# Two 32x32 products per head, moved from two strips of the PE array to four

## The chip, the cores and the metric

The kernel runs on one core of a Trainium2 chip. The metric is the time of one execution on the device, in microseconds (us). A core has TensorE (PE, matrix products; its weight loads are listed as PEld), VectorE (DVE), ScalarE (ACT), GpSimd (POOL) and SyncE (SP). SP, ACT and POOL also issue DMAs, each from a queue of its own. Every engine takes its instructions in order.

## The reference

The inputs are q, k, v of 4 batches, 8 heads, 768 tokens and 48 features, and beta. Per batch and head a delta rule runs over the tokens:

```
k_n = k / (norm(k) + 1e-6)
for t in range(S):
    y[t] = q[t] @ state
    state += beta[t] * outer(k_n[t], v[t] - k_n[t] @ state)
```

The 4 x 768 rows of 384 results then pass two layers: `relu(x @ w_in)**2 @ w_out` (384 to 2048 and back), and `max(x @ w1, x @ w2, x @ w3) @ w_out2` (384 to 768 and back).

## The kernel before, in words

The tokens are cut into 12 chunks (c) of 64. Within a chunk the delta rule needs, for each of 32 batch-head pairs, the inverse of a 64x64 triangular matrix with a unit diagonal. The pairs are held as 16 units u, with t = 0, 1 on the partitions: partition 64 t + token, then u.

The inverse is made in halves. `solve32` inverts the two 32x32 diagonal blocks of all pairs of two chunks at once on DVE (`solve`, lines 285 to 288) and stores them to DRAM as `xt` (line 325), one half h after the other. `load_x(c)` fetches them into `xb`: the first half to partitions 64 t to 64 t + 31, columns 0 to 31, the second half to the next 32 partitions, columns 32 to 63 (four DMAs, line 342). It also fetches `k21`, the off-diagonal block of the products of the keys (two DMAs, line 339; chunk 0 has that block in `kss`). For chunk 0 the DMAs are issued by SP and ACT, for the others by POOL.

The missing quarter is merged by two functions of `attention(c)`. `zz` transposes the first halves into `xT` on DVE (line 398), multiplies the second half by the off-diagonal block into `pZ` (line 405, 32 matmuls) and reads `pZ` out with the sign turned (lines 408, 410) into `z`, which is `k21`'s buffer. `ww` multiplies that by the first half into `pW` (line 418, 32 matmuls) and reads it out into `xb`, columns 32 to 63 of the first halves (lines 421, 423). In `pZ` and `pW` the units lie side by side on 32 partitions for each t:

```python
for u in range(B * Q):
    for t in range(2):
        pe.matmul(pW[first(t), u], xT[first(t), u], z[first(t), u], start=True, stop=True)
```

After that `mm_u` (line 449) applies the whole inverse, `st2` makes the outputs and the growth of the state (lines 489, 467), and `st3` transposes into `xh`, `xl`, the input of the first layer. `st0` (lines 428, 439, 442) stands ahead of it. Each runs once for either half p of the units. `load_att` issues on POOL's queue, behind `load_x`, the loads kq, v, p and ktp of a chunk (lines 358 to 366).

The first layer of chunk c (`moe_a(c)`, lines 544 and 562 on PE, 548 to 551 behind it: `gh` on ACT, `gl` on DVE) is interleaved with `attention(c + 1)`: `steps` takes some steps of the attention for each step of the layer, at given rates, and in even chunks a solve for the next two chunks beside them. PSUM holds two buffers for the layer's first product (`p1`), which come free with `gl`. The instruction lists that come out of this text are then ordered for each engine by the framework's planner, which simulates when data are ready. After chunk 11 the second layer runs (lines 849 to 869).

`behind(a, b)` only fixes an order of two instructions. `att` tiles with `bufs=1` have one buffer, which the next chunk takes over.

Of the kernel before, what the change touches and what calls it, by code (L numbers as in the profile page):

```python
# [8 lines left out]
F32 = mybir.dt.float32  # L9
# [4 lines left out]
AF = mybir.ActivationFunctionType  # L14
ALU = mybir.AluOpType
# [3 lines left out]
B, H, S, D = 4, 8, 768, 48  # L19
C = 64  # L20
NC = S // C
Q = H // 2
# [14 lines left out]
U2 = 2 * Q  # L37


def delta_moe(ctx, tc, kc, ab, kt, vt, beta, beta32, beta16, kq, w_in, w_out, w1, w2, w3, w_out2, out):  # L40
    nc = tc.nc
    vec, act, pool, pe = nc.vector, nc.scalar, nc.gpsimd, nc.tensor
# [11 lines left out]
    att = pr.enter_context(tc.tile_pool(name="att", bufs=2, side="right"))  # L54
    ps_at = pp.enter_context(tc.tile_pool(name="ps_at", bufs=3, space=PSUM))
# [12 lines left out]
    xt_d = [dram.tile([2, 2, B * Q, 32, 32], F32, name=f"xt{c}", tag=f"xt{c}") for c in range(NC)]  # L68
# [202 lines left out]
    def behind(ins, before):  # L271

        tc.add_manual_dep(ins, before.name, mybir.DependencyInfo(mybir.DependencyClass.NoSync, mybir.DependencyReason.DATA), reason="order")
# [55 lines left out]
    xb = st.tile([128, B * Q, C], F32, name="xb", tag="xb")  # L329
# [3 lines left out]
    def load_x(c):  # L333

        k21 = att.tile([128, B * Q, 32], F32, name="k21", tag="k21", bufs=1)
        ds = []
        for t in range(2):
            if c:
                ds.append(pool.dma_start(k21[64 * t + 32:64 * t + 64], kk_d[c][32:64, t, :, 0:32]))
            for h in range(2):  # L340
                o, hs = 64 * t + 32 * h, slice(32 * h, 32 * h + 32)
                i = (pool if c else (nc.sync, act)[t]).dma_start(xb[o:o + 32, :, hs], xt_d[c][h, t].rearrange("u j i -> j u i"))
                if c:
                    ds.append(i)
                else:
                    x_loaded.append(i.ins)
        for i in x_after:
            for d in ds:
                behind(d.ins, i)
        return k21  # L350

    def load_att(c, p):
        ds = []
        us = slice(U2 * p, U2 * p + U2)
        kq_ = None
        if c:
            kq_ = att.tile([R2, U2, 2, C], F32, name="kq", tag="kq")
            ds.append(pool.dma_start(kq_, two(kc, c, p).rearrange("p b q t s -> p (b q) t s")))
        v = att.tile([128, U2, D], F32, name="v", tag="v")
        ds.append(pool.dma_start(v, two(vt, c, p).rearrange("p b q d -> p (b q) d")))  # L360
        pt_ = masked.pop((c, p), None)
        if pt_ is None:
            pt_ = att.tile([128, U2, C], F32, name="p", tag="p")
            ds.append(pool.dma_start(pt_, p_d[c][:, us]))
        kt_ = ktp[p]
        ds.append(pool.dma_start(kt_[:, 0:U2 * D], two(kt, c, p).rearrange("p b q d -> p (b q d)")))
        for i in x_after:
            for d in ds:
                behind(d.ins, i)
        tiles[c, p] = [kq_, v, xb[:, us], pt_, kt_, None, None, None, None]  # L370

    xh, xl, masked, last_act, last_vec = {}, {}, {}, [None], [None]
# [3 lines left out]
    def attention(c):  # L376
# [3 lines left out]
        first = lambda t: slice(64 * t, 64 * t + 32)  # L380
        last = lambda t: slice(64 * t + 32, 64 * t + 64)
# [10 lines left out]

        merge = []

        def zz(k21):
            xT = att.tile([128, B * Q, 32], F32, name="xT", tag="xT", bufs=1)
            z = k21
            last_vec[0] = vec.transpose(out=xT, in_=xb[:, :, 0:32]).ins
            if c == 1:
                behind(last_vec[0], last_gl[0])  # L400
            pZ = ps_at.tile([128, B * Q, 32], F32, name="pZ", tag="at")
            for u in range(B * Q):
                for t in range(2):
                    lower = k21[last(t), u] if c else kss[u // U2][last(t), 0, u % U2, 0:32]
                    pe.matmul(pZ[first(t), u], lower, xb[last(t), u, 32:64], start=True, stop=True)  # L405
            for t in range(2):
                if t and not c:
                    last_vec[0] = vec.tensor_scalar(out=z[first(t)], in0=pZ[first(t)], scalar1=-1.0, scalar2=None, op0=ALU.mult).ins
                else:
                    last_act[0] = act.activation(out=z[first(t)], in_=pZ[first(t)], func=AF.Copy, scale=-1.0).ins  # L410
            merge.extend((xT, z))

        def ww(_):
            xT, z = merge
            pW = ps_at.tile([128, B * Q, 32], F32, name="pW", tag="at")
            for u in range(B * Q):
                for t in range(2):
                    pe.matmul(pW[first(t), u], xT[first(t), u], z[first(t), u], start=True, stop=True)  # L418
            for t in range(2):
                if t and not c:  # L420
                    last_vec[0] = vec.tensor_copy(xb[first(t), :, 32:64], pW[first(t)]).ins
                else:
                    last_act[0] = act.copy(xb[first(t), :, 32:64], pW[first(t)]).ins

        def st0(p):
            kq_, v = tiles[c, p][0:2]
# [79 lines left out]
        def st3(p):  # L506
# [6 lines left out]
            last_act[0] = act.copy(hi, pv).ins  # L513
            last_vec[0] = vec.tensor_sub(out=xl[c][:, :, 128 * p:128 * (p + 1)], in0=pv, in1=hi.bitcast(F32)).ins  # L514

        k21 = load_x(c)
        if not c:
            load_att(c, 0)
        load_att(c, 1)
        if c:  # L520
            order = ((st0, 0),), ((zz, k21),), *(((),) if c == 1 else ()), ((ww, 0),), ((mm_u, 0),), ((st2, 0),), ((st0, 1), (st3, 0)), ((mm_u, 1),), ((st2, 1),), ((st3, 1),)
        else:
            order = ((st0, 0), (st0, 1)), ((zz, k21),), ((ww, 0),), ((mm_u, 0), (mm_u, 1)), ((st2, 0), (st2, 1)), ((st3, 0), (st3, 1)), ((state, 0), (state, 1))
        for fs in order:
            for f, p in fs:
                f(p)
                if f is (mm_u if c else state) and p and c + 1 < NC:
                    load_att(c + 1, 0)
            yield
# [121 lines left out]
    if True:  # L651
# [55 lines left out]
        at, p1 = (ps_at, "at"), (ps_s1, "p1")  # L707
# [47 lines left out]
        for f in range(NF):  # L755
            raw = fetch(wi_src[:, :, 256 * f:256 * (f + 1)], (KD, 128), nc.sync)
            t = None
            if f < NE:
                t = pkp.tile([128, KD, 128], I32, name=f"mag{f}", tag=f"mag{f}")
# [12 lines left out]
        for n, _ in zip((0, 2, 1, 1, 1, 1, 1), attention(0)):  # L772
            abs_after[:], cast_after[:] = cast_after or abs_after, [x for x in last_act if x]
            after[:] = [x for x in last_vec if x] or after
            words(n)
            if second_out:
                for x in second_out:
                    behind(nc.sync.dma_start(*x).ins, x_loaded[1])
                second_out.clear()
# [12 lines left out]
        for c in range(NC):  # L792
            extra = []
            if c + 1 < NC:
                extra.append((9 / 15.0, attention(c + 1)) if c > 1 else (13 / 15.0, later(3, attention(1))) if not c else (17 / 15.0, later(8, attention(2))))
# [24 lines left out]
            if c == NC - 1:  # L820
                pr.close()
                wb = ctx.enter_context(tc.tile_pool(name="wb", bufs=1, side="right", reuse_waits="tile"))
                first = []
# [117 lines left out]
```

## Time and profile before

| | |
|---|---|
| median of 3 runs | 995.46 us (994.43 to 995.75) |
| profiled execution | 997.21 us, its span 995.5 us |
| PE busy | 914.8 us, 92% of the span |
| DVE busy | 454.8 us, 46% |
| ACT busy | 420.1 us, 42% |
| POOL busy | 129.5 us, 13% |
| granted PE clock, mean | 0.958 of 2.4 GHz |
| DMA packets | 74916, of them 35520 under 512 B |

Times are of one profiled execution; the span runs from the first to the last instruction. A busy PE counts matmuls that overlap in the pipeline once. The name k in rows of the trace stands for the tile k21, p for the tile p or p1.

### The profile page before, as it was taken

Reading aid. Unit: us, or ns where it says so; the run is one execution under the profiler, and the core shown is the slowest. Engines: PE = TensorE matmul, PEld = TensorE weight load, DVE = VectorE, ACT = ScalarE, POOL = GpSimd, SP = SyncE. Lnnn points to the kernel's source line nnn. Section 1 sums busy time; section 2 is a strip of 40 time slices with the busy share of each in tenths; the row PEclk is TensorE's granted clock in tenths of the full one; section 3 lists DMA queues with packets and bytes.
Section 4 is the critical chain, followed back from the end, with each engine's and each line's share of the span. In section 5 each row is a group of like instructions: output and inputs, shape, how many; then the busy total and the mean of one; then the engine's idle time right before and its main releaser. Section 6 shows DMA issues by size and latency. Waiting matters only on the chain.

```text
span 995.5 us, 26545 instructions
## 1 busy us (share of the span) xinstructions
PE 914.8 (92%) x11674; PEld 841.1 (84%) x11674; DVE 454.8 (46%) x976; ACT 420.1 (42%) x805; POOL 129.5 (13%) x213
## 2 busy tenths in 40 slices
PE   5067878999999989999999799999999999999998
PEld 4057868999999989999999699999888888888887
DVE  2968577239423832384248234456732323232221
ACT  1946883444444444544444356555421212121111
POOL 3122311121121112112211111000200000000000
PEclk8567998999999999999999899999999999999999
DMA  9938822651564145414531532224500100000001
GB/s 203 315 87 246 238 71 62 150 163 53 135 163 103 53 133 150 117 53 134 150 80 55 138 100 78 66 80 127 159 9 16 47 16 32 16 17 16 12 21 40
DMA packets 74916, 97.25 MB, mean 98 GB/s; under 512 B 35520, under 2 KB 53232, under 8 KB 74800
## 3 DMA queue, kind: packets, MB, share of 16 engines
q1 hardware_dynamic: 54688, 54.22, 19.6%
q0 software_dynamic: 11584, 34.90, 12.6%
q10 hardware_dynamic: 8528, 6.42, 2.2%
q8 instruction: 92, 1.51, 0.7%
q14 instruction: 24, 0.20, 0.1%
HBM read 70.88 MB, written 24.64 MB: 96 GB/s over the span
## 4 chain that ended last, share of the span: by engine, by line
PE 69%; DVE 10%; issue 8%; DMA 6%; ACT 5%; POOL 1%; ACTq 0%; POOLq 0%; SPq 0%; DVEq 0%
PE p L849 23%; PE p L544 15%; PE px L562 15%; PE po L866 8%; DVE buf L287 3%; DVE buf L285 3%; DMA xb<-xt 2%; PE pU L449 2%; PE pZ L405 1%; DMA v<-in_vt_dram 1%; PE pY L489 1%; PE pW L418 1%; DMA xt<-buf 1%; PE pk L197 1%; DVE gl L551 1%
## 5 line engine op out<-in xcount | busy, mean ns | idle before, releaser
L562 PE MATMUL px<-gh,wout 128*128 128x256 f32 x1152 | 221.8, 290 | 1.7 <-issue 1.1
L849 PE MATMUL p<-x_h,w 128*128 128x512 f32 x648 | 203.5, 395 | 0.0
L562 PEld LDWEIGHTS px<-gh,wout 128*128 128x128 f32 x1152 | 181.6, 194 | 5.4 <-issue 1.0
L544 PE MATMUL p<-xh,win_h 128*128 128x256 f32 x576 | 170.5, 297 | 6.3 <-DVE gl L551 4.6
L544 PE MATMUL p<-xl,win_h 128*128 128x256 f32 x576 | 166.3, 292 | 2.8 <-DVE xl L514 2.8
L544 PE MATMUL p<-xh,win_l 128*128 128x256 f32 x576 | 165.5, 288 | 0.0
L562 PE MATMUL px<-gl,wout 128*128 128x256 f32 x576 | 163.9, 284 | 0.0
L849 PEld LDWEIGHTS p<-x_h,w 128*128 128x128 f32 x648 | 121.8, 188 | 27.0
L551 DVE TENSOR_TENSOR gl<-p,gh 128x512 fp32r<-128x512 f32 x96 | 65.7, 686 | 146.3 <-ACT gh L550 145.3
L849 PE MATMUL p<-x_l,w 128*128 128x512 f32 x324 | 128.1, 395 | 0.0
L548 ACT ACTIVATE p<-p 128x512 f32<-128x512 f32 x96 | 55.9, 582 | 156.8 <-PE p L544 155.6
L544 PEld LDWEIGHTS p<-xh,win_h 128*128 128x128 f32 x576 | 113.3, 197 | 10.1 <-DVE gl L551 5.5
L544 PEld LDWEIGHTS p<-xl,win_h 128*128 128x128 f32 x576 | 112.8, 197 | 3.9 <-DVE xl L514 2.9
L544 PEld LDWEIGHTS p<-xh,win_l 128*128 128x128 f32 x576 | 113.5, 197 | 0.1
L562 PEld LDWEIGHTS px<-gl,wout 128*128 128x128 f32 x576 | 111.4, 193 | 0.2 <-DVE gl L551 0.2
L855 DVE TENSOR_TENSOR mx<-p,mx 128x512 f32<-128x512 f32 x36 | 24.9, 691 | 127.2 <-PE p L849 127.1
L857 ACT CAST hh<-mx 128x512 fp32r<-128x512 f32 x36 | 22.3, 620 | 126.6 <-DVE mx L856 126.6
L849 PEld LDWEIGHTS p<-x_l,w 128*128 128x128 f32 x324 | 61.0, 188 | 14.5
L287 DVE TENSOR_TENSOR buf<-buf 128x30 f32<-128x30 f32 (+9 forms) x180 | 59.5, 331 | 5.2
L285 DVE TENSOR_TENSOR buf<-buf 128x30 f32<-128x30 f32 (+9 forms) x180 | 59.4, 330 | 5.4
L550 ACT CAST gh<-p 128x512 fp32r<-128x512 f32 x96 | 56.2, 585 | 2.7
L549 ACT ACTIVATE p<-p 128x512 f32<-128x512 f32 x96 | 55.9, 582 | 2.8
(171 smaller groups left out, 1338.1 us busy)
## 6 DMA issues: line engine op xcount, KB each, us to landing
kq<-in_kc_dram POOLq DMA_DIRECT2D x22, 448.0 KB, 4.4
raw<-in_moe_w_dram SPq DMA_DIRECT2D x18, 384.0 KB, 3.3
p<-p POOLq DMA_DIRECT2D x22, 256.0 KB, 3.3
raw<-in_moe_w_out_dram SPq DMA_DIRECT2D x14, 384.0 KB, 3.7
v<-in_vt_dram POOLq DMA_DIRECT2D x24, 192.0 KB, 4.2
ktp<-in_kt_dram POOLq DMA_DIRECT2D x24, 192.0 KB, 3.4
xr<-x SPq DMA_DIRECT2D x12, 384.0 KB, 3.1
out_dram<-os ACTq DMA_DIRECT2D x24, 192.0 KB, 1.9
```

Source lines behind the costliest of these rows:

```text
L285: eng.tensor_tensor(out=tv, in0=M[:, 0:j, j].unsqueeze(2).broadcast_to([u, j, m]), in1=M[:, j, j + 1:n].unsqueeze(1).broadcast_to([u, j, m ...
L287: yield eng.tensor_tensor(out=M[:, 0:j, j + 1:n], in0=M[:, 0:j, j + 1:n], in1=tv, op=ALU.add)
L544: pe.matmul(p1[:, j], w[:, k, f], x[c][:, k], start=n == 0 and j == 0, stop=n == 8, skip_group_check=True)
L548: act.activation(out=p1, in_=p1, func=AF.Relu)
L549: act.activation(out=p1, in_=p1, func=AF.Square)
L550: last_gh[0] = act.copy(gh, p1).ins
L551: last_gl[0] = vec.tensor_sub(out=gl, in0=p1, in1=gh.bitcast(F32)).ins
L562: pe.matmul(acc[m], w, x[:, j], start=f == 0 and i == 0 and m != 1, stop=f == NF - 1 and i == 2, skip_group_check=True)
L849: pe.matmul(p, w[i][:, k, fs], x[:, k], start=n == 0, stop=n == 8)
L855: vec.tensor_max(out=t, in0=ps[1], in1=t)
L857: act.copy(hh[:, f], t2)
L866: pe.matmul(po[:, 0:DM], x[:, f, js], w[:, f], start=i == 0, stop=i == 17)
```

## The change

Half of the units (u from 8 to 15) move beside the others on the partitions: `pZ`, `pW`, `xT` and `z` now have 8 units on 128 partitions instead of 16 on 64. Each matmul writes one of four 32-column strips; in `ww` it also reads from one of four 32-row strips. The order of the units alternates between the two groups. `z` is read out of `pZ` by one instruction on ACT instead of two, `pW` by four instead of two. As `xT` is now transposed from tiles on 128 partitions, the first halves are loaded a second time into a new tile `x1` in that layout, by four DMAs a chunk behind those of `xb`; the transpose takes `x1` instead of `xb`.

```diff
+        x1 = att.tile([128, U2, 32], F32, name="x1", tag="x1", bufs=1)
...
+        for t in range(2):
+            for g in range(2):
+                o = 64 * t + 32 * g
+                i = (pool if c else (nc.sync, act)[t]).dma_start(x1[o:o + 32], xt_d[c][0, t, U2 * g:U2 * g + U2].rearrange("u j i -> j u i"))
+                ds.append(i)
         for i in x_after:
-            for d in ds:
-                behind(d.ins, i)
-        return k21
+            if c:
+                for d in ds:
+                    behind(d.ins, i)
+        return k21, x1
...
+        part_ = lambda t, u: slice(64 * t + 32 * (u // U2), 64 * t + 32 * (u // U2) + 32)
+        spread = [u for v in range(U2) for u in (v, v + U2)]
+
+        def zz(k21, x1):
+            xT = att.tile([128, U2, 32], F32, name="xT", tag="xT", bufs=1)
+            z = k21[:, 0:U2]
+            last_vec[0] = vec.transpose(out=xT, in_=x1).ins
...
+            pZ = ps_at.tile([128, U2, 32], F32, name="pZ", tag="at")
+            for u in spread:
                 for t in range(2):
                     lower = k21[last(t), u] if c else kss[u // U2][last(t), 0, u % U2, 0:32]
-                    pe.matmul(pZ[first(t), u], lower, xb[last(t), u, 32:64], start=True, stop=True)
-            for t in range(2):
-                if t and not c:
-                    last_vec[0] = vec.tensor_scalar(out=z[first(t)], in0=pZ[first(t)], scalar1=-1.0, scalar2=None, op0=ALU.mult).ins
-                else:
-                    last_act[0] = act.activation(out=z[first(t)], in_=pZ[first(t)], func=AF.Copy, scale=-1.0).ins
+                    pe.matmul(pZ[part_(t, u), u % U2], lower, xb[last(t), u, 32:64], start=True, stop=True)
+            last_act[0] = act.activation(out=z, in_=pZ, func=AF.Copy, scale=-1.0).ins
...
-            for u in range(B * Q):
+            for u in spread:
                 for t in range(2):
-                    pe.matmul(pW[first(t), u], xT[first(t), u], z[first(t), u], start=True, stop=True)
-            for t in range(2):
-                if t and not c:
-                    last_vec[0] = vec.tensor_copy(xb[first(t), :, 32:64], pW[first(t)]).ins
-                else:
-                    last_act[0] = act.copy(xb[first(t), :, 32:64], pW[first(t)]).ins
+                    pe.matmul(pW[part_(t, u), u % U2], xT[part_(t, u), u % U2], z[part_(t, u), u % U2], start=True, stop=True)
+            for g in range(2):
+                for t in range(2):
+                    to, po = xb[first(t), U2 * g:U2 * g + U2, 32:64], pW[part_(t, U2 * g)]
+                    if t and not c:
+                        last_vec[0] = vec.tensor_copy(to, po).ins
+                    else:
+                        last_act[0] = act.copy(to, po).ins
```

U2 is 8. `zz` gets both tiles; nothing else in the order of the steps changes.

## Rows read from the trace of the kernel before

**Rows 1.** The page: an engine's busy us, share of the span, instructions
```profile
PE 914.8 (92%) x11674; PEld 841.1 (84%) x11674; DVE 454.8 (46%) x976; ACT 420.1 (42%) x805; POOL 129.5 (13%) x213
```

**Rows 2.** Busy us by stage: from:to, length, engines (instructions), clock, DMA share, GB/s
```profile
0.00:70.00 70.00, 24.02 (x529) 22.60 (x529) 42.13 (x104) 33.49 (x53) 17.23 (x36) 0.63 0.80 206
70.00:160.00 90.00, 71.79 (x1195) 66.39 (x1199) 68.03 (x164) 62.36 (x120) 23.41 (x40) 0.89 0.55 166
160.00:262.00 102.00, 100.79 (x1783) 95.38 (x1783) 53.45 (x131) 45.94 (x94) 20.69 (x34) 1.00 0.45 120
...
361.00:460.00 99.00, 98.14 (x1741) 94.03 (x1741) 46.98 (x113) 44.35 (x91) 17.95 (x29) 0.98 0.41 111
```

**Rows 3.** Waits, 160 to 690 us: waiter, releaser: us, times, longest
```profile
PE pZ L405 <- DMA xb<-xt: 6.6, 1, 6.6
PE p L544 <- DVE gl L551: 4.3, 5, 2.5
...
DVE xT L398 <- DMA xb<-xt: 39.9, 9, 8.9
DVE v L428 <- DMA v<-in_vt_dram: 27.2, 13, 3.9
...
POOL xb L342 <- PE pU L449: 11.0, 5, 4.0
```

**Rows 4.** Groups by line: form, count | busy us, mean ns | idle before
```profile
L342 POOL DMA_DIRECT2D xb<-xt x44 | 28.6, 658 | 53.6 <-DMA xt<-buf 26.6 <-issue 16.0 <-PE pU L449 11.0
...
L418 PE MATMUL pW<-k,xT 32*32 32x32 f32 x768 | 15.7, 196 | 1.1 <-ACT k L410 0.7 <-DVE k L408 0.4
...
L410 ACT ACTIVATE k<-pZ 32x512 f32<-32x512 f32 x23 | 13.5, 587 | 12.9 <-PE pZ L405 12.6
...
L423 ACT COPY xb<-pW 32x512 f32<-32x512 f32 x23 | 13.2, 575 | 15.2 <-PE pW L418 15.0
...
L454 ACT COPY u<-pU 128x384 f32<-128x384 f32 x23 | 11.1, 481 | 40.2 <-PE pU L449 40.2
...
L398 DVE STREAM_TRANSPOSE xT<-xb 128x512 f32<-128x512 f32 x12 | 8.5, 711 | 39.9 <-DMA xb<-xt 39.9
```

**Rows 5.** Timeline of PE, a block of pW in chunk 6: start, length
```profile
373.34 1.20 PE L418 MATMUL pW<-k,xT 32*32 32x32 f32 x64
```

**Rows 6.** Busy us of L439 alone, then of L449 alone: PE, PEld, clock
```profile
437.00:440.00 3.00, 1.15 (x64) 1.02 (x64) 1.00 0.02 5
...
442.00:444.00 2.00, 1.13 (x32) 1.01 (x32) 1.00 0.44 122
```

**Rows 7.** Timeline of DVE at the transpose of chunk 6
```profile
360.40 0.71 DVE L398 STREAM_TRANSPOSE xT<-xb 128x512 f32<-128x512 f32 x1 [5.73 <-DMA xb<-xt]
361.03 1.25 DVE L551 TENSOR_TENSOR gl<-p,gh 128x512 fp32r<-128x512 f32 x2
```

**Rows 8.** Timeline of POOL, the loads of chunk 6
```profile
324.69 1.34 POOL L339 DMA_DIRECT2D k<-kk  x2 [5.14 <-ACT xb L423]
...
355.64 2.62 POOL L342 DMA_DIRECT2D xb<-xt  x4 [7.08 <-DMA xt<-buf]
358.25 0.55 POOL L358 DMA_DIRECT2D kq<-in_kc_dram  x1
```

**Rows 9.** Chain that ended last: start, us; then busy by stage, as rows 2
```profile
361.74 3.11 PE p L544 x18
...
368.92 2.34 PE p L544 x18
...
361.70:364.80 3.10, 3.06 (x19) 3.06 (x20) 1.74 (x3) 0.00 (x0) 0.00 (x0) 0.73 0.90 258
```

**Rows 10.** Timeline of chunk 0's merge on DVE and PE
```profile
59.53 0.69 DVE L408 TENSOR_SCALAR k<-pZ 32x512 f32<-32x512 f32 x1 [3.64 <-ACT k L410]
60.27 1.91 PE L418 MATMUL pW<-k,xT 32*32 32x32 f32 x62 [0.41 <-DVE k L408]
```

More of the change, by code (lines that the diff above doesn't have):

```diff
@@ L393, in attention @@
         merge = []
[L395 to L398, printed above, removed]
+        part_ = lambda t, u: slice(64 * t + 32 * (u // U2), 64 * t + 32 * (u // U2) + 32)
[4 more added lines that the diff above has]
+            last_vec[0] = vec.transpose(out=xT, in_=x1).ins
             if c == 1:
                 behind(last_vec[0], last_gl[0])
-            pZ = ps_at.tile([128, B * Q, 32], F32, name="pZ", tag="at")
-            for u in range(B * Q):
+            pZ = ps_at.tile([128, U2, 32], F32, name="pZ", tag="at")
+            for u in spread:
                 for t in range(2):
                     lower = k21[last(t), u] if c else kss[u // U2][last(t), 0, u % U2, 0:32]
-                    pe.matmul(pZ[first(t), u], lower, xb[last(t), u, 32:64], start=True, stop=True)
-            for t in range(2):
-                if t and not c:
-                    last_vec[0] = vec.tensor_scalar(out=z[first(t)], in0=pZ[first(t)], scalar1=-1.0, scalar2=None, op0=ALU.mult).ins
-                else:
-                    last_act[0] = act.activation(out=z[first(t)], in_=pZ[first(t)], func=AF.Copy, scale=-1.0).ins
+                    pe.matmul(pZ[part_(t, u), u % U2], lower, xb[last(t), u, 32:64], start=True, stop=True)
+            last_act[0] = act.activation(out=z, in_=pZ, func=AF.Copy, scale=-1.0).ins
             merge.extend((xT, z))
@@ L414, in ww @@
             xT, z = merge
-            pW = ps_at.tile([128, B * Q, 32], F32, name="pW", tag="at")
-            for u in range(B * Q):
+            pW = ps_at.tile([128, U2, 32], F32, name="pW", tag="at")
+            for u in spread:
                 for t in range(2):
-                    pe.matmul(pW[first(t), u], xT[first(t), u], z[first(t), u], start=True, stop=True)
-            for t in range(2):
-                if t and not c:
-                    last_vec[0] = vec.tensor_copy(xb[first(t), :, 32:64], pW[first(t)]).ins
-                else:
-                    last_act[0] = act.copy(xb[first(t), :, 32:64], pW[first(t)]).ins
+                    pe.matmul(pW[part_(t, u), u % U2], xT[part_(t, u), u % U2], z[part_(t, u), u % U2], start=True, stop=True)
[6 more added lines that the diff above has]
+                        last_act[0] = act.copy(to, po).ins
         def st0(p):
@@ L514, in st3 @@
             last_vec[0] = vec.tensor_sub(out=xl[c][:, :, 128 * p:128 * (p + 1)], in0=pv, in1=hi.bitcast(F32)).ins
-        k21 = load_x(c)
+        k21, x1 = load_x(c)
         if not c:
@@ L520, in attention @@
         if c:
-            order = ((st0, 0),), ((zz, k21),), *(((),) if c == 1 else ()), ((ww, 0),), ((mm_u, 0),), ((st2, 0),), ((st0, 1), (st3, 0)), ((mm_u, 1),), ((st2, 1),), ((st3, 1),)
+            order = ((st0, 0),), ((zz, (k21, x1)),), *(((),) if c == 1 else ()), ((ww, 0),), ((mm_u, 0),), ((st2, 0),), ((st0, 1), (st3, 0)), ((mm_u, 1),), ((st2, 1),), ((st3, 1),)
         else:
-            order = ((st0, 0), (st0, 1)), ((zz, k21),), ((ww, 0),), ((mm_u, 0), (mm_u, 1)), ((st2, 0), (st2, 1)), ((st3, 0), (st3, 1)), ((state, 0), (state, 1))
+            order = ((st0, 0), (st0, 1)), ((zz, (k21, x1)),), ((ww, 0),), ((mm_u, 0), (mm_u, 1)), ((st2, 0), (st2, 1)), ((st3, 0), (st3, 1)), ((state, 0), (state, 1))
         for fs in order:
             for f, p in fs:
-                f(p)
+                f(*p) if f is zz else f(p)
                 if f is (mm_u if c else state) and p and c + 1 < NC:
```

## Prediction

> **What bounds the kernel now.** I read the page first, then a table of busy time by stage, then who waits for whom, and only then the merge itself. The page gives TensorE (PE) 92% of the span [rows 1]. An average says little, so the table by stage comes next [rows 2]: PE is busy 24.0 of the first 70 us, 71.8 of the next 90, and from 160 us on practically always (100.8 of 102, 98.1 of 99). The granted clock there is 1.00 and 0.98, the 2.4 GHz level. So three stages have three limits. Up to 70 us a chain of small steps for chunk 0 sets the time; from 70 to 160 us PE shares the limit with the weight conversions; from 160 us PE is the bound, and each us of PE work taken out there should shorten the run by about one us, as long as no wait opens in its place.
>
> The waits between 160 and 690 us confirm it [rows 3]: PE waits 6.6 us once for the load of xb, 4.3 us in five places for gl, which VectorE (DVE) writes, and almost nothing else. The same view shows where trouble can come from: DVE stands 39.9 us in nine places before the transpose that begins the merge, waiting for xb, and 27.2 us for v. DVE takes its instructions in order, so what stands behind the transpose (gl above all, on which PE's second matmul and the release of a PSUM buffer depend) waits too.
>
> **The merge on PE.** Per chunk it is two blocks, pZ and pW, of 32 matmuls each; an f32 matmul leaves two records, so 64 records a block, 768 of pW in 12 chunks [rows 4]. Undisturbed, a block of pW covers 1.20 us, and one of pZ as much [rows 5]. The last record alone lasts 0.20 us [rows 4], so 63 gaps share 1.00 us: 16 ns each, or 32 ns for the pair of records that the two tiles (t = 0, 1) start together.
>
> The change spreads the outputs over four 32-column strips. pZ then uses four tiles (two row strips, each with two column strips of its own) and pW four tiles on the diagonal. Does PE run four at once? The trace has the same comparison one size up [rows 6]. L439 (pA and pY) uses all four 64x64 tiles, two row strips by two column strips, and puts 64 records into 1.15 us; L449 (pU) uses two 64x64 tiles and needs 1.13 us for 32 records. Four tiles thus do twice the work of two in one time, and two tiles that share a row strip do not hinder each other, which is the pattern of the new pZ. By that row a block of 64 records takes 16 steps of 32 ns with its tail, 0.50 + 0.20 = 0.70 us, which saves 0.50 us (an estimate; bounds: 0 if the tiles do not overlap, 0.50 if they do, since a tile's own 32 ns stays). From 160 us on there are ten chunks (2 to 11) with two blocks each: 20 x 0.50 = **10.0 us**.
>
> The Trainium skill has a rule that speaks against this: TensorE: Matmul & The Clock Gate, section on 56 ns against 53.3 ns, says that start-to-start of matmuls never falls below about 25 ns however small they are. By it 64 records would need 1.6 us and the change would save nothing; the trace already shows 16 ns, and 15 ns in L439, so here it does not hold across tiles.
>
> **Evictions.** Z was read out by two instructions of 32x512 (587 ns on ACT each), W by two of 575 [rows 4]. Now Z takes one of 128x256 and W four of 32x256. ACT rows of 512 and 384 elements take 587 and 481 ns [rows 4], 0.83 ns an element, so 256 elements come to 0.37 us (an estimate; bounds: half of 0.587 and all of it). ACT: 2.32 us before, 5 x 0.37 = 1.85 us after, 0.5 us less a chunk. The transpose falls from 128x512 (711 ns) to 128x256: between 0.36 and 0.71 us, I take 0.4. From 160 us on neither engine is the bound (their time lies beside PE's matmuls of the other chain), so I count nothing; without that cover Z's read-out would gain 0.8 us a chunk and W's lose 0.35.
>
> **Chunk 0.** Here everything is in series and PE is at the low clock (W's 62 records take 1.91 us [rows 10], 27 ns apart instead of 16). Each block saves half of the 27 x 62 ns, 0.8 us, together 1.7 (bounds 0 and 1.7). Z's read-out ran on ACT (0.59 [rows 4]), and only then on DVE (0.69 [rows 10]): 1.3 us become 0.37, a gain of 0.9. W's took the same 1.3; as four instructions in turn on ACT and DVE (0.37, and 0.42 as an estimate between half and all of 0.69) it is 1.7, a loss of 0.4. Sum: 2.2 us. Against it, the transpose now needs x1, loaded behind xb by two more issues on each of two queues; should that land 1 us late for W, 1.2 us remain. Since the stage to 160 us is not PE's alone, I let 1.0 us of this, and of the 0 to 1.0 us in chunk 1, come through: bounds 0 and 3.2.
>
> **The extra loads.** Chunks 1 to 11 get four more DMAs on POOL's queue. An issue of the kind xb<-xt costs 658 ns there [rows 4], so four cost 2.6 us (the nearest cheaper issue is kq's 0.55 [rows 8], which makes it 2.2). Queued behind them are kq, v, p and ktp of the second pair, of which only v has someone waiting (DVE, 27.2 us in all [rows 3]; PE does not stand for it). Who waits for x1 itself is the transpose, and through DVE's order gl.
>
> In odd chunks xt is long in memory, and x1, unlike xb, need not wait until the previous chunk's pU has read its buffer (xb waited 11.0 us for that in five places [rows 3]). Its loads can go early, and the transpose then hangs on x1 alone: no loss, and a DVE wait may vanish. In the five even chunks from 2 on, xt is stored just before. There xb's four issues start at 355.64 and kq's issue follows at 358.25 [rows 8]; the transpose runs at 360.40 after 5.7 us of idle DVE, and two gl come right behind it [rows 7]. If the order on POOL is xb, then x1, and DVE keeps its order, the transpose runs 2.6 us later and so do both gl. PE then stands longer: in this chunk it already waited for gl, and afterwards ran at a granted clock of 0.73 [rows 9].
>
> The instruction order is not the text's, though: the two k21 loads stand among xb's in the text and are issued together 31 us ahead of them [rows 8]. A planner orders each queue by when it believes data to be ready, and when it sees x1 land later it can put one or both gl ahead of the transpose; then PE stands less than now. So the bounds for the even chunks are -4 us (all waits of PE for gl vanish) and +13.0 us (5 x 2.6). Of the 39.9 us that DVE stood before transposes only 4.3 reached PE, a tenth, which of 13.0 would be 1.4; but where PE already waits (2.5 of the 4.3 us lie in one place [rows 3]) a later transpose counts in full, 2.6. I take the sum of the two less what a better order may save, **+3 us**.
>
> **Sum.** -10.0 - 1.0 + 3.0 = -8.0 us. The profiled execution lasted 997.21 us (span 995.5 and 1.7 around it), 0.18% over the median of the runs, so 997.2 becomes 989.2; from the median, 995.46 becomes **987.5 us**. A measurement here tells about 0.2% (2 us) from no change.
>
> **Rivals.**
> - *The x1 loads eat it.* All five even chunks keep DVE's order, the transpose comes 2.6 us later each time: +13.0, and the clock that falls after a longer stand costs too (18 matmuls of p took 3.11 us after the stand against 2.34 later [rows 9], 0.8 us each time, 4 in all). -11.0 + 13.0 + 2 to 4 is 4 to 6 us slower, 1000.5 us. It decides from 2.2 us of new PE stall per even chunk on. For it: PE's waits for gl are exactly there. Against it: only a tenth of DVE's standing reached PE so far, so there is slack.
> - *The four tiles do not overlap.* Then PE's 10.0 us are not there and only side effects remain: -1 + 3, 997.5 us, with bounds of 991 and 1005. Against it: L439 beside L449. For it: no row shows four tiles of 32x32, nor four row strips writing one bank. A milder form halves only pW: two row strips into one bank are seen in pW today, four are not; 5.0 us less gain, 992.5 us. The Trainium skill, TensorEngine Tiling (Array Packing), Gotcha 1 on PSUM pressure, says that different row tiles cannot use one PSUM bank at the same time; by it pW's four tiles would take turns, the milder form. In L439 two row strips write pA's bank side by side at full rate, so this trace does not bear it out.
> - *The new order removes waits as well.* The transposes of odd chunks run early, gl passes the even ones: -10.0 - 1 to -3 - 4: 979 to 981 us.
>
> **How the numbers follow.** Forecast, with the even chunks' cost between 0 and 7 us (984 to 992): 0.56. New order also removes waits (under 984): 0.10. x1 loads eat part of it (992 to 997.5, with the milder bank case): 0.16. They eat all of it: 0.12. No overlap: 0.06. Faster by over 0.2% (under 993.5) takes the first two and a third of the next, 0.71; within 0.2% the rest of that case and half of no overlap, 0.13; slower 0.16. The likeliest case's own range is 984 to 992; the range for 8 in 10 reaches to part of both other sides, 980 to 999.
>
> **What would show it.** Blocks of L405 and L418 of 0.70 us instead of 1.20, with 64 records each; if they stay at 1.2, the overlap is refuted. PE's busy time from 160 to 690 us down by about 10 us. L410 one per chunk at 0.37 us, L423 four of 0.37. 44 issues of x1<-xt on POOL, 32 KB each, at about 0.6 us, early in odd chunks and behind xb's in even ones. The page's packets under 512 B rise by about a third (12 chunks x 4 DMAs x 256 rows of 128 bytes). PE's waits for gl in the even chunks tell how the 3 us went: above 15 us in all, the first rival is right. What would make the prediction wrong: a planner that orders other work anew, so that a wait opens at a place that the change does not touch.

## The result, and the profile after

The changed kernel takes 987.32 us (median of 4 runs, 983.45 to 987.65) against 995.1 us before (994.43 to 995.75), a ratio of 0.9903 with an interval of 0.9878 to 0.9929. Timed a second time it had 987.72 us and a ratio of 0.9922. The change is worth 0.8 to 1.0%, 8 to 10 us. The profiled execution is its fastest, 983.45 us with a span of 981.7, while the one before lay 0.18% over its median; so the two traces differ by 13.8 us, of which some 4 to 6 are the choice of runs, and no place in them is to be read to the microsecond.

The page after, which answers to [rows 1], with its lines on traffic:

```profile
PE 902.9 (92%) x11674; PEld 830.0 (85%) x11674; DVE 452.8 (46%) x976; ACT 414.3 (42%) x817; POOL 154.1 (16%) x257
...
DMA packets 77413, 98.84 MB, mean 101 GB/s; under 512 B 37312, under 2 KB 55024, under 8 KB 77296
```

PE is busy 11.9 us less with the same 11674 matmuls. POOL is busy 24.6 us more, ACT 5.8 less. The groups of the merge, answering to [rows 4] (line 351 loads x1, which the trace calls x; 408 is the transpose, 415 and 424 are pZ and pW, 416 and 431 their read-outs on ACT):

```profile
L351 POOL DMA_DIRECT2D x<-xt x44 | 25.5, 586 | 13.5 <-DVE xT L408 12.7 <-issue 0.7
...
L431 ACT COPY xb<-pW 32x256 f32<-32x256 f32 x46 | 16.7, 364 | 10.1 <-PE pW L424 8.7 <-DVE xb L429 0.8
...
L424 PE MATMUL pW<-k,xT 32*32 32x32 f32 x768 | 9.6, 198 | 0.8 <-DVE xT L408 0.7
...
L408 DVE STREAM_TRANSPOSE xT<-x 128x256 f32<-128x256 f32 x12 | 5.3, 445 | 23.1 <-DMA x<-xt 21.4 <-PE pW L424 1.7
L416 ACT ACTIVATE k<-pZ 128x256 f32<-128x256 f32 x12 | 4.6, 386 | 23.7 <-PE pZ L415 18.5 <-DMA kq<-in_kc_dram 5.3
```

One record still lasts as long (198 ns against 196), but 768 of pW now cover 9.6 us instead of 15.7: more of them run at once. Two blocks that nothing else interrupts (62 of the 64 records of a pZ, and a whole pW), which answer to [rows 5], show it directly:

```profile
459.46 0.74 PE L415 MATMUL pZ<-xb,k 32*32 32x32 f32 x62 [0.41 <-DMA xb<-xt]
...
563.61 0.75 PE L424 MATMUL pW<-k,xT 32*32 32x32 f32 x64
```

0.75 us instead of 1.20, 0.45 us a block. The waits of 160 to 690 us, answering to [rows 3]:

```profile
PE p L552 <- DVE gl L559: 3.1, 3, 2.7
PE pZ L415 <- DMA xb<-xt: 2.6, 4, 1.2
PE pU L457 <- DVE xl L522: 1.8, 1, 1.8
...
DVE xT L408 <- DMA x<-xt: 18.1, 5, 6.1
```

DVE stands 18.1 us before the transpose instead of 39.9, and PE's one wait of 6.6 us for xb has become four of 2.6 in all. A new one stands beside them, 1.8 us for xl.

To see where the time went I divided both spans at the same places of the program: the ends of the first layer of chunks 0, 1, 3 and 11. First the kernel before, then the one after (columns as in [rows 2]):

```profile
0.00:147.00 147.00, 85.64 (x1595) 79.63 (x1595) 98.38 (x238) 91.98 (x164) 39.65 (x73) 0.78 0.70 192
147.00:207.20 60.20, 56.49 (x1000) 53.22 (x1001) 29.52 (x68) 23.66 (x46) 10.97 (x19) 0.94 0.47 123
207.20:305.00 97.80, 97.26 (x1743) 92.82 (x1742) 46.77 (x111) 45.79 (x93) 17.96 (x29) 1.00 0.49 129
305.00:689.40 384.40, 373.19 (x5937) 357.14 (x5936) 187.12 (x424) 189.80 (x382) 53.88 (x87) 0.99 0.36 98
```

```profile
0.00:140.60 140.60, 80.00 (x1539) 74.99 (x1543) 94.20 (x227) 90.12 (x163) 40.63 (x75) 0.78 0.73 203
140.60:202.50 61.90, 54.47 (x938) 51.44 (x938) 31.72 (x76) 22.83 (x46) 13.52 (x24) 0.89 0.41 114
202.50:305.10 102.60, 100.93 (x1871) 96.53 (x1872) 47.67 (x113) 46.74 (x101) 25.61 (x42) 0.97 0.49 132
305.10:675.90 370.80, 365.26 (x5937) 348.84 (x5936) 185.80 (x424) 185.75 (x389) 67.70 (x111) 1.00 0.37 104
```

The first three rows are to be read together: in the change PE has some 60 records less in each of the first two and 128 more in the third, as the attention's work lies otherwise beside the layer. Up to 305 us the two kernels are level: PE's work fell by 4.0 us (239.4 to 235.4, the first three rows added), its idle time rose by as much (65.6 to 69.7). From there on the change gains 13.6 us: 7.9 of work, 5.7 of idle time. That stretch holds the merges of chunks 5 to 11, 14 blocks; at 0.45 us they make 6.3 of the 7.9; the rest fits the clock (0.99 and 1.00), but was not taken apart. The idle time is two places: PE's stand of 2.47 us for gl in chunk 6 is gone, and the one of 6.6 us for xb in chunk 10 is now 2.7 for gl and 0.6 for xb. In the trace of the change once more, a run of 987.37 us and so near the median, that stand is 3.8 us, all of it for gl.

Of the loss before 305 us one place is plain, chunk 3's second half. DVE's order, before and after:

```profile
195.81 0.55 DVE L514 TENSOR_TENSOR xl<-pT,xh 128x384 fp32r<-128x384 f32 x1
201.52 0.56 DVE L428 TENSOR_TENSOR v<-v,normT 128x384 f32<-128x384 f32 x1 [3.40 <-DMA v<-in_vt_dram]
```

```profile
198.50 0.56 DVE L436 TENSOR_TENSOR v<-v,normT 128x384 f32<-128x384 f32 x1 [4.42 <-DMA v<-in_vt_dram]
198.98 0.55 DVE L522 TENSOR_TENSOR xl<-pT,xh 128x384 fp32r<-128x384 f32 x1
```

Before, xl ran ahead of v and nobody waited. Now v, whose load POOL issues at 194.38 us (196.18 before), stands ahead of it, DVE waits 4.4 us for that load, and PE idles 1.84 us until 199.59 for xl.

### The profile page after: what moved, and what is told of

Same layout as the page of the kernel before. It is cut to its first block, busy times and chain, and to the rows that moved or that the text cites. A ratio compares the mean times of both kernels' runs of the same rounds, so it can differ in the third digit from the quotient of the medians.

```text
span 981.7 us, 26638 instructions
## 1 busy us (share of the span) xinstructions
PE 902.9 (92%) x11674; PEld 830.0 (85%) x11674; DVE 452.8 (46%) x976; ACT 414.3 (42%) x817; POOL 154.1 (16%) x257
## 2 busy tenths in 40 slices
DMA packets 77413, 98.84 MB, mean 101 GB/s; under 512 B 37312, under 2 KB 55024, under 8 KB 77296
## 4 chain that ended last, share of the span: by engine, by line
PE 69%; DVE 10%; DMA 8%; issue 6%; ACT 4%; POOL 2%; ACTq 0%; SPq 0%; DVEq 0%; POOLq 0%
PE p L857 23%; PE p L552 15%; PE px L570 14%; PE po L874 8%; DVE buf L287 3%; DVE buf L285 3%; PE pU L457 2%; DMA xb<-xt 2%; PE pY L497 2%; DMA v<-in_vt_dram 1%; DMA buf<-kk 1%; DMA xt<-buf 1%; PE pZ L415 1%; PE pk L197 1%; PE pW L424 1%
## 5 line engine op out<-in xcount | busy, mean ns | idle before, releaser
L570 PE MATMUL px<-gh,wout 128*128 128x256 f32 x1152 | 218.8, 289 | 1.2 <-issue 1.2
L857 PEld LDWEIGHTS p<-x_l,w 128*128 128x128 f32 x324 | 61.0, 188 | 14.5
```

The source lines that it names most:

```text
L570: pe.matmul(acc[m], w, x[:, j], start=f == 0 and i == 0 and m != 1, stop=f == NF - 1 and i == 2, skip_group_check=True)
L857: pe.matmul(p, w[i][:, k, fs], x[:, k], start=n == 0, stop=n == 8)
```

## The experiments

My theory (A) was the prediction's: PE is the bound, four tiles side by side save their share of PE time, the loads cost a few us. The rivals: (B) the gain comes from another order of the work, or from fewer DVE waits, and not from the overlap; (C) it comes from chunk 0, where everything is in series. Each kernel was timed in five rounds beside the kernel before; the ratio is to that. The medians are from different chips, so where two of these kernels are compared below, the ratios are taken, of 996 us; the intervals are 1 to 3 us to either side.

| kernel | median us | ratio, 95% interval |
|---|---|---|
| the change, units in order | 997.24 | 1.0007 (0.9991 to 1.0024) |
| before, with the loads of x1 that nobody reads | 1009.78 | 1.0136 (1.0123 to 1.0149) |
| the change in chunk 0 alone | 998.39 | 1.0026 (1.0014 to 1.0038) |
| the change in all chunks but 0 | 988.50 | 0.9902 (0.9877 to 0.9926) |
| the change without x1, four transposes from xb | 993.41 | 0.9981 (0.9969 to 0.9994) |
| the change, pZ in order, pW alternating | 992.48 | 0.9943 (0.9920 to 0.9967) |
| the change, x1 behind xb in even chunks | 979.97 | 0.9819 (0.9794 to 0.9845) |
| the change, x1 by two loads | 993.27 | 0.9952 (0.9929 to 0.9976) |
| before, transpose behind gl in even chunks | 993.49 | 0.9971 (0.9955 to 0.9987) |
| x1 by two loads, transpose behind gl | 986.34 | 0.9900 (0.9871 to 0.9928) |
| the same, and x1 behind xb | 988.58 | 0.9926 (0.9903 to 0.9950) |

**Units in order.** All of the change but the alternation: two neighbouring units write the same strips, so only two tiles run at once.

```diff
-        spread = [u for v in range(U2) for u in (v, v + U2)]
+        spread = range(B * Q)
```

> The changed kernel with one line undone: the units run in the order 0 to 15 in both blocks, so that neighbouring matmuls use two tiles (t = 0, 1) and not four; layout, loads, transposes and read-outs stay, and the instructions of DVE, ACT, POOL and SP keep their order. Theory A (the gain is four tiles running side by side on PE): blocks of pZ and pW return from 9 to 16 ns a record, 0.45 us each, 20 blocks from 160 us on and some of chunk 0: 9 to 11 us slower than the changed kernel, about 997 us. Theory B (the gain comes from the shorter read-outs and transposes, from chunk 0's chain and from DVE waiting less): no change, about 987 us.

997.24 us: no gain at all. The other engines' instructions stand in the same order as in the change, so the two kernels differ by the overlap alone, and 0.9903 or 0.9922 against 1.0007 is 8.5 to 10.4 us of overlap. (B) falls as the cause of the gain: order, loads and read-outs together come to nothing. Its block of pW, and its two long stretches, divided as above:

```profile
521.59 1.11 PE L424 MATMUL pW<-k,xT 32*32 32x32 f32 x64
```

```profile
206.50:310.30 103.80, 102.59 (x1872) 98.11 (x1872) 47.95 (x113) 46.76 (x101) 25.55 (x42) 0.96 0.50 130
310.30:689.60 379.30, 373.19 (x5937) 356.60 (x5936) 185.80 (x424) 185.75 (x390) 67.69 (x111) 0.99 0.38 102
```

It is 5.3 us behind the kernel before at 310 us and has won 5.1 back by 690, with no less work on PE (373.19 as before). That it is the loads that cost early and the new order that gives back later fits this, but is not shown apart.

**The loads alone.** The kernel before, with x1 loaded by the lines of the change and read by nobody.

```diff
+        x1 = att.tile([128, U2, 32], F32, name="x1", tag="x1", bufs=1)
...
+                ds.append(i)
         for i in x_after:
-            for d in ds:
-                behind(d.ins, i)
+            if c:
+                for d in ds:
+                    behind(d.ins, i)
```

> The kernel before with the four loads of x1 a chunk added and nothing that reads them: everything else is as before. The prediction's term for the extra loads is +3 us with bounds of -4 and +13, so 998.5 us. If the loads are hidden: 995.5 us. If the planner puts them between the two halves of xb in even chunks, as it did in the changed kernel, pZ's data land about 2.3 us later there, which PE sees only where it stands for them: 0 to 5 us.

1009.78 us, 13.6 more: a little over the prediction's upper bound for the loads (13.0), and more than any of the three expectations. Its dearest place is the merge of chunk 3. The transpose, still from xb, waits for its load; behind it on DVE stands Sb (the state, with its growth added), for which PE idles 2.76 us until 215.00. The three views are DVE's timeline, PE's waits from 155 to 690 us, and the stretch after the stand:

```profile
213.70 0.71 DVE L405 STREAM_TRANSPOSE xT<-xb 128x512 f32<-128x512 f32 x1 [6.33 <-DMA xb<-xt]
214.33 0.52 DVE L481 TENSOR_TENSOR Sb<-pD,Sb 128x384 f32<-128x384 f32 x1
```

```profile
PE p L551 <- DVE gl L558: 9.2, 6, 6.2
PE pU L456 <- DVE xl L521: 2.9, 1, 2.9
PE pT L517 <- DVE Sb L481: 2.8, 1, 2.8
```

```profile
215.00:225.00 10.00, 10.00 (x105) 9.07 (x105) 1.89 (x4) 3.11 (x6) 0.00 (x0) 0.69 0.48 134
```

After this stand, the second in a short time (2.95 us until 206.83, for xl), PE worked 10 us at a clock of 0.69, so the stands cost more than their own length. The loads are not cheap in this order of the work; in the change the transpose no longer hangs on xb, and the order differs.

**Chunk 0 alone, and all but chunk 0.** A flag chooses the old or the new functions, and x1 is loaded only where the new ones run.

```diff
...
+        zz, ww = (zz_new, ww_new) if not c else (zz_old, ww_old)
```

> The new merge in chunk 0 alone, the old one in chunks 1 to 11, with x1 loaded for chunk 0 only. The prediction let 1.0 us of chunks 0 and 1 come through: about 994.5 us. The trace of the changed kernel is 6.5 us ahead at the end of chunk 0's layer; should that be chunk 0's merge and should it last, about 989 us; should it be a timing of loads that either kernel can meet, 993 to 995 us.

> The complement of the run with chunk 0 alone: the old merge in chunk 0, the new one in chunks 1 to 11. Chunk 0 alone cost 2.2 us. If the two parts add up, this one is 10 us faster than before, about 986 us, better than the whole change. If chunk 0's shorter chain does come through in the whole change, as the prediction had it (1.0 of 2.2 us), it is 988 to 990 us.

Chunk 0 alone is slower by 2.6 us (1.4 to 3.8), which none of the three expectations had; all but chunk 0 has the whole gain, so (C) falls. The prediction's 1.0 us does not show in chunk 0 alone; the run without chunk 0 can't tell so little, as its interval is 2.4 us to either side. Chunk 0's own chain did become shorter. From pZ's start to the second transposes of st3 it lasts 14.70 us before and 11.95 in the change:

```profile
56.96 1.00 PE L405 MATMUL pZ<-xb,buf 32*32 32x32 f32 x29 [0.87 <-DMA xb<-xt]
...
71.66 0.52 PE L510 MATMUL pT<-ident,yy 128*128 128x128 f32 x3 [0.90 <-DVE yy L502]
```

```profile
56.90 0.27 PE L415 MATMUL pZ<-xb,buf 32*32 32x32 f32 x2 [32.80 <-DMA xb<-xt]
...
68.85 0.52 PE L518 MATMUL pT<-ident,yy 128*128 128x128 f32 x3 [0.51 <-DVE yy L510]
```

At the end of pU the change is 2.3 us ahead; the rest comes behind the merge, where the clock rose earlier (from 66.3 to 68.85 us it is 1.00, and 0.50 before). Chunk 0 alone, divided as above, shows what became of that:

```profile
0.00:146.00 146.00, 85.37 (x1596) 79.62 (x1596) 97.83 (x238) 91.88 (x166) 39.77 (x73) 0.77 0.71 195
146.00:209.10 63.10, 56.88 (x1001) 53.57 (x1001) 29.61 (x68) 23.69 (x47) 10.93 (x18) 0.95 0.44 117
```

1.0 us is left at the end of the first layer's first chunk, and the second chunk takes 2.9 us more (63.1 against 60.2, PE idle 6.2 against 3.7). In part the chain only started later in this trace: pZ at 58.94 us, 2.0 later than before, and already SP's store of xt, which stands ahead of the changed part, is issued at 51.10 instead of 49.67. Why the second chunk waits longer was not followed further.

**No second load.** x1 goes; four transposes of 32x256 take the first halves straight from xb.

```diff
...
-            last_vec[0] = vec.transpose(out=xT, in_=x1).ins
...
+            for t in range(2):
+                for g in range(2):
+                    last_vec[0] = vec.transpose(out=xT[part_(t, U2 * g)], in_=xb[first(t), U2 * g:U2 * g + U2, 0:32]).ins
...
```

> The changed kernel without x1: four transposes of 32x256 on DVE take the first halves from xb and write xT in the spread layout. It saves four issues of 0.58 us on POOL a chunk and costs DVE some 1.2 us a chunk (four transposes of about 0.4 instead of one). If the second loads cost the 3 us that the prediction gave them: 984 us. If they are hidden: 987 us. If the transposes of odd chunks, which now wait for xb again, hold gl up: 988 to 992 us.

993.41 us, by the ratios 6 to 8 slower than the change though it has the overlap and fewer loads. What its trace shows is DVE's order, here in chunk 6:

```profile
360.87 1.78 DVE L405 STREAM_TRANSPOSE xT<-xb 32x256 f32<-32x256 f32 x4 [4.86 <-DMA xb<-xt]
362.69 1.29 DVE L556 TENSOR_TENSOR gl<-p,gh 128x512 fp32r<-128x512 f32 x2
```

The transposes, four times 435 ns, stand ahead of both gl, as in [rows 7], and PE waits for gl in chunks 4, 6, 8 and 10: 2.85, 2.81, 1.62 and 6.63 us (the last stands where PE stood 6.6 us for xb before). The change at the same place, DVE and then POOL (which answers to [rows 8]):

```profile
356.85 0.69 DVE L559 TENSOR_TENSOR gl<-p,gh 128x512 fp32r<-128x512 f32 x1 [3.48 <-ACT gh L558]
359.37 0.45 DVE L408 STREAM_TRANSPOSE xT<-x 128x256 f32<-128x256 f32 x1 [1.83 <-DMA x<-xt]
359.74 0.65 DVE L559 TENSOR_TENSOR gl<-p,gh 128x512 fp32r<-128x512 f32 x1
```

```profile
354.11 1.33 POOL L343 DMA_DIRECT2D xb<-xt  x2 [6.84 <-DMA xt<-buf]
355.43 2.30 POOL L351 DMA_DIRECT2D x<-xt  x4
357.72 1.29 POOL L343 DMA_DIRECT2D xb<-xt  x2
```

One gl has passed the transpose, which DVE awaits 1.8 us instead of 5.7. But x1's four issues stand between the halves of xb, so the second halves, for which pZ waits, come 2.3 us later.

**Only pW side by side.** pZ keeps the old order of units.

```diff
-            for u in spread:
+            for u in range(B * Q):
                 for t in range(2):
                     lower = ...
```

> The changed kernel with pZ's units in order (two tiles at a time) and pW's still alternating (four). Both in order cost about 10 us. If either block gives its half: about 992 us. If pW's four row strips, which write one bank, were no faster, all the gain would be pZ's and this would be 997 us.

992.48 us. Against the units in order (0.9943 and 1.0007) pW's alternation alone brings 6.4 us of the 8.5 to 10.4; pZ's brings the other 2 to 4. Either block carries its share, and at intervals of 1.6 to 2.4 us that is not clear of one half each. A block of pW has its new length, with four row strips that write one PSUM bank:

```profile
519.45 0.75 PE L424 MATMUL pW<-k,xT 32*32 32x32 f32 x64
```

**x1 behind xb.** In even chunks x1's loads come after all four of xb (`i` is then the last load of xb).

```diff
+        xb_last = i
...
+                if c and not c % 2:
+                    behind(i.ins, xb_last.ins)
```

> The changed kernel with the four x1 loads of even chunks held behind xb's last one on POOL; the planner had put them between the two halves of xb. pZ's data then land 2.3 us earlier in even chunks and the transpose 1.3 us later. If PE's remaining waits for xb (2.6 us in four places) are the price of that order: 1 to 3 us faster than the changed kernel, about 985 us. If a later transpose holds gl up, the prediction's first rival: 990 to 995 us.

979.97 us (978.93 to 981.18), 1.8% faster than before and, by the ratios, 0.8 to 1.0% than the change: the best version found. POOL and DVE in chunk 6, and its long last stretch up to the end of the first layer, divided as above:

```profile
354.80 2.61 POOL L343 DMA_DIRECT2D xb<-xt  x4 [7.38 <-DMA xt<-buf]
357.40 2.30 POOL L352 DMA_DIRECT2D x<-xt  x4
```

```profile
357.01 0.69 DVE L562 TENSOR_TENSOR gl<-p,gh 128x512 fp32r<-128x512 f32 x1 [3.48 <-ACT gh L561]
358.92 0.69 DVE L562 TENSOR_TENSOR gl<-p,gh 128x512 fp32r<-128x512 f32 x1 [1.22 <-ACT gh L561]
...
363.02 0.45 DVE L411 STREAM_TRANSPOSE xT<-x 128x256 f32<-128x256 f32 x1 [2.81 <-DMA x<-xt]
```

```profile
305.20:671.10 365.90, 362.93 (x5938) 347.16 (x5936) 185.97 (x424) 185.70 (x389) 67.69 (x111) 1.00 0.39 106
```

xb's second halves go first, and the planner now puts both gl ahead of the transpose, presumably as it sees x1 land later. The transpose runs 3.7 us later than in the change, and PE does not stand for it: of the stretch's 365.9 us PE idles 3.0, against 5.5 in the change and 11.2 before. Two things changed at once, the place of xb's loads and that of the transpose; no run parts them with four loads.

**The change once more**, unaltered, beside the last kernels below.

> The changed kernel itself once more, beside the three below on one chip, because the runs of the other experiments spread by some us. By its first comparison, a ratio of 0.990 to the kernel before, about 987 us.

987.72 us, 0.9922 (0.9900 to 0.9945), which agrees with the first time within the intervals.

**Half as many loads.** Even and odd units take the two groups, so x1 needs two DMAs of 64 partitions instead of four.

```diff
...
+            i = (pool if c else (nc.sync, act)[t]).dma_start(x1[64 * t:64 * t + 64], xt_d[c][0, t].rearrange("(v g) j i -> (g j) v i", g=2))
...
+        part_ = lambda t, u: slice(64 * t + 32 * (u % 2), 64 * t + 32 * (u % 2) + 32)
+        spread = range(B * Q)
...
```

> The changed kernel with even and odd units in the two groups instead of units 0 to 7 and 8 to 15: x1 then comes by two DMAs of 64 partitions a chunk instead of four of 32, the matmuls run in the order 0 to 15 on four tiles, and W is read out with a stride of two units. It saves two issues of 0.58 us on POOL a chunk. The loads alone cost the kernel before 13.6 us; if that grows with the number of issues, 2 to 5 us faster than the changed kernel, 983 to 985 us. If it is their place in the order that costs, no change, about 987 us.

993.27 us, by the ratios 3 to 5 slower than with four loads; I had expected a gain. One issue now costs 693 ns, so POOL needs 1.4 us a chunk instead of 2.3, and yet:

```profile
362.13 0.45 DVE L406 STREAM_TRANSPOSE xT<-x 128x256 f32<-128x256 f32 x1 [6.56 <-DMA x<-xt]
362.50 1.25 DVE L557 TENSOR_TENSOR gl<-p,gh 128x512 fp32r<-128x512 f32 x2
```

With the load cheaper the transpose stands ahead of both gl again, DVE waits 6.6 us for x1, and PE 3.0 for gl (in all 6.7 in five places, and 4.9 for xb in chunk 10). The order on DVE would then outweigh the time on the queue; the next runs test that.

**The order by hand.** If that is right, holding the transpose behind gl must help the kernel before, and mend the version with two loads:

```diff
-            if c == 1:
+            if c and (c == 1 or not c % 2):
                 behind(last_vec[0], last_gl[0])
```

> The kernel before with one line added: in even chunks the transpose stands behind the latest gl on DVE instead of ahead of it. Merge, loads and read-outs are those of before. If the place of the transpose is what PE's waits for gl hang on (4.3 us in five places, and the lower clock after the longest), and not the merge on two tiles: 3 to 6 us faster than before, 990 to 993 us. If the changed kernel's smaller waits came from its shorter transposes and read-outs: no change, 996 us.

> The kernel with x1 in two loads, which was slower than the changed one (0.995 of before against 0.990) although it issues less: there the planner put the transpose ahead of both gl again, since it saw x1 ready earlier. Here the transpose is put behind gl. If that place was the loss: 5 to 8 us faster than with two loads alone, 984 to 987 us. If two loads are slower in themselves: still about 992 us.

The kernel before gains 3 us (0.9971; 1.3 to 4.5 us) without any other edit, the version with two loads 5 (0.9952 to 0.9900, in two sessions), which makes it as fast as the change. PE's waits in the former, from 155 to 690 us:

```profile
PE pZ L405 <- DMA xb<-xt: 6.2, 1, 6.2
...
PE p L544 <- DVE gl L551: 1.1, 2, 0.8
```

gl's 4.3 us [rows 3] are down to 1.1; the wait for xb in chunk 10 stays. In the latter they are down from 6.7 to 0.4. Both remedies together, on two loads:

```diff
...
+            if c and not c % 2:
+                behind(i.ins, xb_last.ins)
```

> As the one with two loads and the transpose behind gl, and x1's loads also held behind xb's last in even chunks. xb first gave 0.982 of before with four loads. If xb's place and the transpose's place are two separate gains: at least as good, 977 to 980 us, the best version. If xb first only worked by moving the transpose: no better than the run with two loads and the transpose behind gl.

988.58 us: they do not add up. It is no better than with the transpose behind gl alone, as the second expectation had it; but as that place alone reaches 0.9900 and not 0.9819, it is not the whole of what x1 behind xb won. Its PE waits 4.6 us for xb in chunk 10, where the four loads behind xb leave 0.75. What spares that one the wait stays open; so does whether two loads could be brought below 980 us.

## Why the prediction was right

**PE is the bound, and the blocks overlap: right, and the size nearly so.** The blocks went from 1.20 to 0.75 us, not 0.70, as the records are 9 ns apart and not 8 (a tile's own 32 ns did not quite stay: four tiles make 36): 20 x 0.45 = 9.0 us instead of 10.0. Undoing the overlap alone costs 8.5 to 10.4 us, of which the blocks account for 20 x 0.36 = 7.2 (1.11 to 0.75). PE's busy time fell by 11.9 us on the page, since the four blocks of chunks 0 and 1 are in it too.

**Two rules that spoke against it.** The Trainium skill, TensorE: Matmul & The Clock Gate, section on 56 ns against 53.3 ns, has start-to-start never below about 25 ns. Records of different tiles here start 9 ns apart in the mean, so for tiles side by side the measurement decides against it. The Trainium skill, TensorEngine Tiling (Array Packing), Gotcha 1, would have row tiles take turns on one PSUM bank. pW's four row strips share one and keep 0.75 us; the measurement does not bear that out either, and the milder rival falls with it.

**Chunks 0 and 1, -1.0 us: not borne out.** The chain became 2.3 us shorter up to the end of pU, close to the 2.2 of the prediction (whose read-outs of W, 0.37 and 0.42 twice, add up to 1.6 and not 1.7). But nothing of it is seen at the end: chunk 0 alone is 2.6 us slower, and leaving it out changes nothing that these runs can tell. The step that failed is that a part of a gain in series comes through; with chunk 0 alone the next chunk waited longer instead. Chunk 1 was not tested alone.

**The loads, +3.0 us: the size about right, by luck.** All but the overlap comes to +0.7 us (-0.9 to +2.4); as that kernel's blocks are themselves 0.09 us shorter than before (1.11), 1.8 us in 20, the loads and the order cost an estimated 2.5 (PE's work on its page, 913.9 us against 914.8, bears out half of that 1.8). It is the sum of two larger terms: the trace of the units in order loses 5.3 us up to 310 us and wins 5.1 after it. The prediction feared the transposes of the even chunks, as late as x1, and gl behind them; there it went better (PE's waits for gl are 3.1 us in all, 4.3 before), as gl passed the transpose or the transpose came earlier. What it did not see is the early stretch, where v changed places with xl. The same turn stands in the kernel before with the loads alone, and in the one without a second load, but not where chunk 0 alone is changed; so it is not x1's loads only that bring it, and what does stays open. It also placed x1 behind xb in even chunks, while the planner put it between the halves; the version with that order is 8 to 10 us faster than the change.

**The sum.** That the forecast of 987.5 lies within half a us of both medians is luck in part. The overlap, nearly all of the gain, was right in its cause and to about 1 us in its size. But the 9.0 us of the blocks and the 2.5 of the loads make only -6.5, where -7.8 to -9.7 were measured. Intervals of 1 to 3 us leave room for the difference, and no run shows where it lies. The 1.0 us of chunks 0 and 1 did not show at all.

**Read-outs counted at nothing: right as far as shown.** They took 386 and 364 ns where 0.37 us was estimated, the transpose 445 ns for 0.4. ACT lost 5.8 us of work, and no wait of PE for these read-outs is above 0.5 us from 155 to 690 us.

**The rivals.** That the loads eat the gain is what happens in the kernel before (+13.6 us): the mechanism, a transpose in front of other work on DVE, is real, and the version with two loads shows it once more. It did not decide here, where the planner chose another order. That the new order removes waits as well is half true, after 305 us. The forecast of a third more small packets was wrong: 35520 became 37312, 5%.

## What to carry to other kernels

Where PE is the bound, small matmuls can gain from a layout that puts neighbouring instructions on different row and column strips, here also where they write one bank (1.20 to 0.75 us a block); test the order of issue alone, as without alternation nothing was gained here. Where engines work in order, look at what stands behind an instruction that awaits a load: there a cheaper load can be slower (0.9952 against 0.9903) and a later one faster (0.9819). Fixing DVE's order by hand was worth 3 us in the kernel before, and x1 behind xb in POOL's order 8 to 10 on top of the change. A gain in a serial stretch may not reach the end: follow it into the stretch that comes next.

## What was unexpected of the hardware

Four 32x32 tiles of f32 put a record every 9 ns, two tiles every 14.5 to 16 ns, at the clock of 2.4 GHz (granted 1.00); in chunk 0, at the lower level of 1.2 GHz (granted 0.50), 13 and 24 to 27 ns. An issue on POOL's queue costs by its shape: 586 ns for a load of 32 partitions by 8 units, 658 for 32 by 16, 693 for 64 by 8, so two of the last are much cheaper than four of the first. And in the kernel before with the loads alone two stands of PE of under 3 us each, 8 us apart, are followed by 10 us at a mean clock of 0.69; the forecast had priced that at 0.8 us for each stand [rows 9], while at 0.69 it is some 3 us of the 10 (an estimate: 31% of the 10 us).
